# A placement table for the attention steps, half-array score and value matmuls, and reciprocals by Ln and Exp, in an attention and channel-mix kernel

## The chip, the cores and the metric

One core of one Trainium2 chip. The metric is device time in microseconds of one execution: the median of the runs shown. A profiled execution is one more run, recorded by the hardware profiler.

## What is computed

The reference, cut to what matters (B = 8, H = 8, S = 576, D = 64, 32 memory slots; channel mix 512 to 1024 to 512):

```python
a = np.exp(phi - phi.max(axis=2)); a = a / a.sum(axis=2)      # over the sequence
k_m = np.einsum('bhsm,bhsd->bhmd', a, k)
v_m = np.einsum('bhsm,bhsd->bhmd', a, v)
attn = softmax(q @ k_m.T / sqrt(64))                          # over the 32 slots
x = attn @ v_m                                                # to (B, S, 512)
xk = mu_k * x + (1 - mu_k) * x_prev                           # x_prev: one token back
xr = mu_r * x + (1 - mu_r) * x_prev
kk = np.maximum(xk @ w_k, 0)
out = sigmoid(xr @ w_r) * ((kk * kk) @ w_v)
```

## The kernel before

The eight batches go through `attention(b)`, one after the other; the 4608 tokens go through `channel_mix(c)` in nine chunks c0 to c8 of 512 tokens. Chunk c needs the tokens of batches up to c. Each chunk is 16 groups of matmuls on TensorE, one per slot: eight `key` (`pk`, L380, evicted by ScalarE's Relu L385, squared by VectorE L386), four `gate` (`pr`, L393, Tanh on ScalarE L396) and four `value` (`pv`, L404, product `o` on VectorE L407, stored by SP's queue L367). A group is four matmuls of 512 columns, or eight for `value`.

A batch's attention is a list of steps. `exp_phi` exponentiates phi (`em`). `ekv` sums em times k and v, and em times ones (`kvps`, `zps`, L193), two heads in either half of the array's columns. `norm_k` and `norm_v` divide by the sums and mask (`kbd`, `vbd`), `tr_k` and `tr_q` transpose through TensorE (`kmT`, `qT`). `scores` adds two matmuls over the full array (L252) and ScalarE exponentiates (`e`, L254). `zsum` gathers the denominators of all heads in 48 rows (`zcps`, L262), VectorE takes the reciprocal `rzf` in two bf16 parts, `spread` brings them back to 128 rows (`rbps`, L280) and multiplies (`atn`, L285). `values` gives `nops` (L294), copied by ScalarE to `x` (L296). `diff` and `mix` make `xkT` and `xrT` on VectorE (L305 to L318).

The order of work on every engine is the order in which the program issues it. The steps and the groups are interleaved by hand: the plan at the end of `attention` gives each step a slot, from batch 2 on by one plan that is stretched over 15 to 31 slots. `load_batch` puts the loads of k, q and v on POOL's queue, phi of batch 0 on SP's. The PSUM tag "at" with three buffers is shared by all attention steps; "pk" has two, "pv" three.

```python
        first = {2: 0, 3: -8}.get(b, -16)
        return [(15 - (15 - r) * (15 - first) // 31, s) for r, s in plan]
```

Of the kernel before, what the change touches and what calls it, by code (L numbers as in the profile page):

```python
# [13 lines left out]
AL = mybir.AluOpType  # L14

# [7 lines left out]
def kernel(  # L23
# [25 lines left out]
    SEG = 96  # L49
    NSEG = S // SEG  # L50
# [11 lines left out]
    identity = const.tile([128, 128], BF16, name="identity")  # L62
    make_identity(nc, identity)
# [4 lines left out]
    kmTs = [const.tile([128, 2, 2, 128], BF16, name=f"kmT{i}") for i in range(2)]  # L68
# [38 lines left out]
    for i in range(4):  # L107
        fs = slice(i * Dff // 4, (i + 1) * Dff // 4)
        nc.gpsimd.dma_start(out=wk_sb[:, :, fs], in_=wk_v[:, :, fs])
    nc.gpsimd.dma_start(out=wr_sb, in_=moe_w_r.rearrange("(do di) d2 -> di do d2", di=128))  # L110
    nc.gpsimd.dma_start(out=wv_sb, in_=moe_w_v.rearrange("(fo fi) d -> fi fo d", fi=128))
    load_batch(1)
# [8 lines left out]
    maskv = const.tile([128, 2, 2, D], BF16, name="maskv")  # L121
    nc.vector.memset(maskk, 0.0)
    nc.vector.memset(maskv, 0.0)
    for g in range(4):
        r = slice(g * M, (g + 1) * M)
        nc.vector.memset(maskk[r, g % 2, :], 1.0)
        nc.vector.memset(maskv[r, g // 2, g % 2, :], 1.0)

    NROW = H * NSEG
    selz = const.tile([128, 2 * NROW + 128], BF16, name="selz")  # L130
    nc.vector.memset(selz, 0.0)
    for g in range(4):
        nc.vector.memset(selz[g * M:(g + 1) * M, NROW + g * NSEG:NROW + g * NSEG + 1], 1.0)

    LO = 64
    KR = LO + NROW
    sel2 = const.tile([KR, NROW], BF16, name="sel2")
    nc.vector.memset(sel2, 0.0)
    nc.vector.tensor_copy(sel2[:NROW, :], identity[:NROW, :NROW])
    nc.vector.tensor_copy(sel2[LO:KR, :], identity[LO:KR, LO:KR])  # L140
    selb = const.tile([KR, 2, NSEG, 4, M], BF16, name="selb")
    for c in range(2):
        for g in range(4):
            o = c * 4 * NSEG + g * NSEG
            nc.vector.tensor_copy(
                selb[:, c, :, g, :],
                sel2[:, o:o + NSEG].unsqueeze(2).to_broadcast([KR, NSEG, M]))
    rhl2 = [const.tile([KR, SEG], BF16, name=f"rhl{i}") for i in range(2)]
    for t in rhl2:
        nc.vector.memset(t, 0.0)  # L150

    ps_mu = psum.tile([128, 2 * ND], F32, name="psmu", tag="at", bufs=3)
    nc.tensor.transpose(ps_mu, mu2, ident_f)
    mu1 = const.tile([128, 2 * ND], F32, name="mu1")
    nc.vector.tensor_scalar_add(mu1, ps_mu, -1.0)
# [3 lines left out]


    def attention(b):
        st = {}
        kv5, q5, em, kmT = kvs[b % 2], qs[b % 2], ems[b % 2], kmTs[b % 2]
# [5 lines left out]

        def ekv(parts):  # L170

            w = parts.stop - parts.start
            with_z = parts.start == 0

            def go():
                kvps = psum.tile([128, 2, w, 2 * D], F32, name="kvps", tag="at", bufs=3)
                for i in range(w):
                    st["kv"[parts.start + i]] = kvps[:, :, i, :]
                if with_z:
                    st["zps"] = psum.tile([128, 2], F32, name="zps", tag="at", bufs=3)  # L180
                for j in range(NJ):
                    for c in range(2):
                        for what in range(1 + with_z):
                            for jj in range(2):
                                pr = 2 * c + jj
                                lhsT = em[:, j].rearrange("p h m -> p (h m)")[:, pr * 64:(pr + 1) * 64]
                                if what == 0:
                                    rhs = kv5[:, parts, 2 * pr:2 * pr + 2, j, :]
                                    o = kvps[jj * 64:(jj + 1) * 64, c]
                                else:  # L190
                                    rhs = ones
                                    o = st["zps"][jj * 64:(jj + 1) * 64, c:c + 1]
                                nc.tensor.matmul(o, lhsT=lhsT, rhs=rhs, start=j == 0 and c == 0,  # L193
                                                 stop=j == NB, skip_group_check=True)
            return go

        def norm_k():
            rz = work.tile([128, 2], F32, name="rz", tag="rz")
            nc.vector.reciprocal(rz, st["zps"])
            kbd = work.tile([128, 2, 2, D], BF16, name="kbd", tag="kbd")  # L200
            for c in range(2):
                nc.vector.scalar_tensor_tensor(
                    kbd[:, c].rearrange("p h d -> p (h d)"), in0=st["k"][:, c, :],
                    scalar=rz[:, c:c + 1], in1=maskk.rearrange("p h d -> p (h d)"),
                    op0=AL.mult, op1=AL.mult)
            st["kbd"], st["rz"] = kbd, rz

        def norm_v():
            vbd = work.tile([128, 2, 2, 2 * D], BF16, name="vbd", tag="vbd")
            for c in range(2):  # L210
                nc.vector.scalar_tensor_tensor(
                    vbd[:, c], in0=st["v"][:, c].unsqueeze(1).to_broadcast([128, 2, 2 * D]),
                    scalar=st["rz"][:, c:c + 1], in1=maskv.rearrange("p j h d -> p j (h d)"),
# [7 lines left out]
        def tr_k():  # L221
# [5 lines left out]
            for c in range(2):  # L227
                for jj in range(2):
                    nc.vector.tensor_copy(kmT[:, c, jj, jj * 64:(jj + 1) * 64], ps[:, c, jj, :])  # L229
# [15 lines left out]
        def scores(c, hf):  # L245
            def go():
# [10 lines left out]
        def zsum():  # L257
            ps = psum.tile([128, SEG], F32, name="zcps", tag="at", bufs=3)
            for c in range(2):
                for sg in range(NSEG):  # L260
                    o = NROW - (c * 4 * NSEG + sg)
                    nc.tensor.matmul(ps, lhsT=selz[:, o:o + 128],  # L262
                                     rhs=st["e"][:, c, sg * SEG:(sg + 1) * SEG],
                                     start=(c == 0 and sg == 0), stop=(c == 1 and sg == NSEG - 1))
            rzf = work.tile([NROW, SEG], F32, name="rzf", tag="rzf")
            nc.vector.reciprocal(rzf, ps[:NROW, :])
            rhl = rhl2[b % 2]
            nc.vector.tensor_copy(rhl[:NROW, :], rzf)
            nc.vector.tensor_sub(rhl[LO:KR, :], rzf, rhl[:NROW, :])
            st["rhl"] = rhl  # L270

        def spread(c, hf):
            def go():
                if "at" not in st:
                    st["at"] = work.tile([128, 2, S], BF16, name="atn", tag="atn")
                ps = psum.tile([128, HALF], F32, name="rbps", tag="at", bufs=3)
                n = HALF // SEG
                for i in range(n):
                    sg = hf * n + i
                    nc.tensor.matmul(ps[:, i * SEG:(i + 1) * SEG],  # L280
                                     lhsT=selb[:, c, sg].rearrange("p g m -> p (g m)"),
                                     rhs=st["rhl"], start=(i == 0), stop=(i == n - 1),
                                     skip_group_check=True)
                sl = slice(hf * HALF, (hf + 1) * HALF)
                nc.vector.tensor_mul(st["at"][:, c, sl], st["e"][:, c, sl], ps)  # L285
            return go

        def values(pr, hf):
            def go():
                if "x" not in st:  # L290
                    st["x"] = work.tile([128, ND, S], BF16, name="x", tag="x")
                sl = slice(hf * HALF, (hf + 1) * HALF)
                ps = psum.tile([128, HALF], F32, name="nops", tag="at", bufs=3)
                nc.tensor.matmul(ps, lhsT=st["vbd"][:, pr // 2, pr % 2, :],  # L294
                                 rhs=st["at"][:, pr // 2, sl], start=True, stop=True)
                nc.scalar.copy(st["x"][:, pr, sl], ps)  # L296
# [23 lines left out]

        if b <= 1:
            at = [-1] * 5 if b == 0 else [9, 11, 12, 13, 14]
            plan = [
                (at[0] - 3, exp_phi), (at[0], ekv(slice(0, 1))), (at[0], norm_k), (at[0], tr_k),
                (at[1], tr_q(0)), (at[1], tr_q(1)), (at[1], scores(0, 0)), (at[1], scores(0, 1)),
# [93 lines left out]
    def steps_of(b):  # L421
        if b not in made:
            made[b] = attention(b)
# [41 lines left out]
```

## Time and profile before

| | |
|---|---|
| median of 3 runs | 274.89 us (274.87 to 275.49) |
| profiled execution, its own time | 274.43 us |
| its span, first to last instruction | 272.7 us |
| mean granted TensorE clock | 0.947 |
| matmuls / vector / scalar instructions | 1708 / 491 / 221 |

The span is what the profile's rows add up to; 1.7 us of the execution's own time lie outside it. Busy time counts what an engine executes, without waits; matmuls are pipelined, so the spacing of their starts tells their cost better than their durations, which include the way through the array.

### The profile page before, as it was taken

To read this page: it belongs to the slowest core of one execution; us is meant where nothing else is said; L and a number is where in the kernel's file an instruction comes from. 1 tells how busy PE (TensorE), PEld (TensorE's weight loads), DVE (VectorE), ACT (ScalarE), POOL (GpSimd) and SP (SyncE) were. 2 spreads that over 40 slices of the span, in tenths; PEclk is the share of its full clock that TensorE was granted. 3 is DMA by queue.
4 is the path that set the end of the run, shared out by engine and by line. 5 is a ranking of instruction groups with operands and counts; after the bars stand their busy time and mean duration, and the time that the engine had idled before them with its cause. 6 is when DMAs were issued, how large, how long until landed. Compare 5 with 4: busy or idle time off the path is not lost.

```text
span 272.7 us, 4541 instructions
## 1 busy us (share of the span) xinstructions
PE 227.4 (83%) x1708; PEld 117.1 (43%) x1737; DVE 169.8 (62%) x491; ACT 105.3 (39%) x221; POOL 54.4 (20%) x74
## 2 busy tenths in 40 slices
PE   0576798973999985998968897899899999999992
PEld 0442244530455442554535454545454554444441
DVE  7548743549655498545883778378829957933422
ACT  3023263130454513534525343634362472451720
POOL 8552365400262062051202400000000000000000
PEclk9996589996699998899999999999999999999998
DMA  8999999994359779739840991013001401402124
GB/s 149 187 197 217 220 223 192 244 228 74 89 67 185 176 100 188 138 35 192 150 126 2 138 237 41 0 41 105 12 2 40 114 4 38 115 9 110 38 52 102
DMA packets 49653, 31.22 MB, mean 115 GB/s; under 512 B 14824, under 2 KB 44016, under 8 KB 49632
## 3 DMA queue, kind: packets, MB, share of 16 engines
q0 software_dynamic: 42544, 20.91, 55.9%
q1 hardware_dynamic: 7088, 10.03, 13.1%
q8 instruction: 13, 0.21, 0.3%
q14 instruction: 8, 0.07, 0.1%
HBM read 38.28 MB, written 9.44 MB: 175 GB/s over the span
## 4 chain that ended last, share of the span: by engine, by line
PE 54%; DVE 23%; ACT 8%; DMA 8%; issue 5%; POOL 1%; SPq 0%; DVEq 0%; POOLq 0%
PE pk L380 17%; PE pv L404 15%; PE pr L393 8%; DMA out_dram<-o 5%; ACT x L296 4%; PE qtps L238 3%; DMA q<-in_q_dram 3%; DVE o L407 3%; DVE mu_d L317 3%; PE kvps L193 3%; PE scps L252 3%; ACT rl L385 3%; DVE sq L386 2%; DVE diff L305 2%; DVE xkT L318 2%
## 5 line engine op out<-in xcount | busy, mean ns | idle before, releaser
L380 PE MATMUL pk<-xkT,wk 128*128 128x512 bf16 x276 | 75.6, 407 | 9.8 <-DVE xkT L318 8.7
L385 ACT ACTIVATE rl<-pk 128x512 bf16<-128x512 f32 x72 | 42.5, 595 | 73.7 <-PE pk L380 69.5
L404 PE MATMUL pv<-wv,sq 128*128 128x512 bf16 x278 | 66.7, 379 | 0.5
L407 DVE SCALAR_TENSOR_TENSOR o<-th,pv 128x512 f32<-128x512 f32 x36 | 24.6, 684 | 41.1 <-PE pv L404 28.4
L380 PEld LDWEIGHTS <-wk 128*128 128x128 bf16 x288 | 27.5, 102 | 43.3 <-issue 18.5
L386 DVE TENSOR_TENSOR sq<-rl 128x512 bf16<-128x512 bf16 x72 | 29.8, 423 | 26.2 <-ACT rl L385 25.9
L404 PEld LDWEIGHTS <-sq 128*128 128x128 bf16 x288 | 27.7, 98 | 29.3 <-issue 0.2
L396 ACT ACTIVATE th<-pr 128x512 f32<-128x512 f32 x36 | 21.4, 596 | 43.9 <-PE pr L393 43.9
L393 PE MATMUL pr<-wr,xrT 128*128 128x512 bf16 x137 | 35.0, 379 | 0.8 <-issue 0.6
L296 ACT CAST x<-nops 128x288 bf16<-128x288 f32 x64 | 22.1, 407 | 14.5 <-PE nops L294 14.2
L317 DVE TENSOR_SCALAR mu_d<-diff,mu 128x576 bf16<-128x576 bf16 x64 | 22.0, 376 | 0.5
L254 ACT ACTIVATE e<-scps 128x288 bf16<-128x288 f32 x32 | 11.7, 408 | 23.6 <-PE scps L252 23.3
L393 PEld LDWEIGHTS <-xrT 128*128 128x128 bf16 x144 | 13.6, 98 | 14.9 <-issue 0.6
L238 PE MATMUL qtps<-identity,q 128*64 128x128 bf16 x320 | 15.0, 245 | 4.8 <-DVE qT L242 2.3
L252 PE MATMUL scps<-qT,kmT 128*128 128x288 bf16 x64 | 12.9, 315 | 6.4 <-DVE kmT L229 4.9
L238 PEld LDWEIGHTS <-q 128*64 128x64 bf16 x320 | 11.9, 125 | 12.4 <-issue 12.0
L242 DVE COPY qT<-qtps 128x576 bf16<-128x576 bf16 x32 | 13.3, 450 | 5.0 <-PE qtps L238 4.8
L83 POOL DMA_DIRECT2D kv<-in_k_dram x8 | 7.2, 902 | 45.0 <-PE zps L193 42.5
L294 PE MATMUL nops<-atn,vbd 128*128 128x288 bf16 x64 | 14.8, 301 | 1.5 <-ACT x L296 0.6
L193 PE MATMUL kvps<-kv,em 128*64 128x256 bf16 (+1 forms) x200 | 14.9, 272 | 1.0 <-DMA kv<-in_k_dram 0.9
L193 PEld LDWEIGHTS <-em 128*64 128x64 bf16 x360 | 12.9, 120 | 6.1 <-issue 5.5
L285 DVE TENSOR_TENSOR atn<-e,rbps 128x288 bf16<-128x288 bf16 x32 | 12.7, 447 | 1.0 <-PE rbps L280 1.0
(61 smaller groups left out, 196.3 us busy)
## 6 DMA issues: line engine op xcount, KB each, us to landing
out_dram<-o SPq DMA_DIRECT2D x40, 128.0 KB, 2.4
kv<-in_k_dram POOLq DMA_DIRECT2D x8, 512.0 KB, 7.4
q<-in_q_dram POOLq DMA_DIRECT2D x8, 512.0 KB, 9.6
kv<-in_v_dram POOLq DMA_DIRECT2D x8, 512.0 KB, 11.2
out_dram<-o SPq DMA_DIRECT2D x16, 256.0 KB, 3.0
phm<-in_phi_dram POOLq DMA_DIRECT2D x7, 512.0 KB, 10.6
wk<-in_moe_w_k_dram POOLq DMA_DIRECT2D x4, 256.0 KB, 10.8
wv<-in_moe_w_v_dram POOLq DMA_DIRECT2D x1, 1024.0 KB, 15.5
```

The costliest lines, as they stand in the source:

```text
L193: nc.tensor.matmul(o, lhsT=lhsT, rhs=rhs, start=j == 0 and c == 0, stop=j == NB, skip_group_check=True)
L238: nc.tensor.matmul(ps[i * D:(i + 1) * D, j * 128:(j + 1) * 128], lhsT=q5[:, 2 * pr + i, j, :], rhs=identity, is_transpose=True, start=True ...
L252: nc.tensor.matmul(ps, lhsT=kmT[:, c, jj, :], rhs=st["qT"][:, 2 * c + jj, sl], start=(jj == 0), stop=(jj == 1))
L296: nc.scalar.copy(st["x"][:, pr, sl], ps)
L317: nc.vector.tensor_scalar_mul(t[:, i], st["d"][:, pr + i, :], mu1[:, o:o + 1])
L380: nc.tensor.matmul(pk, lhsT=wk_sb[:, di, fi * 128:(fi + 1) * 128], rhs=xk_T[:, di, t0:t0 + CT], start=(di == 0), stop=(di == ND - 1))
L385: nc.scalar.activation(rl, pk, AF.Relu, scale=0.5 ** 0.5)
L386: nc.vector.tensor_mul(st["sq"][:, fi, :], rl, rl)
L393: nc.tensor.matmul(pr, lhsT=xr_T[:, di, t0 + ts * 128:t0 + (ts + 1) * 128], rhs=wr_sb[:, di, :], start=(di == 0), stop=(di == ND - 1))
L396: nc.scalar.activation(th, pr, AF.Tanh, scale=0.5)
L404: nc.tensor.matmul(pv, lhsT=st["sq"][:, fi, ts * 128:(ts + 1) * 128], rhs=wv_sb[:, fi, :], start=(fi == 0), stop=(fi == NF - 1))
L407: nc.vector.scalar_tensor_tensor(o, in0=st["pr"][ts], scalar=1.0, in1=pv, op0=AL.add, op1=AL.mult)
```

## The change

- Every attention step gets a slot from a table: STEADY for batches 4 to 7, FIRST for batches 0 to 3. All groups and steps are sorted by slot. The plan's stretching goes.
- `scores`: the two matmuls of a pair go to two halves of the array's columns, with 64-column weights; kmT is a tile without zeros, copied at once.
- `denom`, `recip`, `weigh`: a matmul by a block matrix of ones (`sumh`) gives each row its denominator; ScalarE takes Ln, then Exp of its negative; VectorE multiplies. `zsum` and `spread` go.
- `values`: vbd is a plain 64-column tile, and the matmuls of a pair read the two halves of the rows.
- `gate`: Exp per group, and for two groups together Ln(x + 1) and Exp of its negative, in place of Tanh; `value` multiplies by it. The factors of one half in Relu and Tanh go.
- em's sums are made in a step of their own (`esum`), with full-width weights.
- At the start: k, then q in two halves, the identity, v in two halves; w_k in two loads; one load of the table with Ln and Exp; sixteen matmuls on zeros (`keep_busy`). The last value group is computed and stored in two halves.

```diff
+STEADY = [("q0", -15), ("q3", -15), ("q2", -15), ("q1", -15), ("exp", -15), ("kv", -14), ("z", -14), ("nk",
...
+    nc.scalar.preload_act_table_set("natural_log_exp_and_others")
...
+    load_phi(0, nc.sync)
+    load_rows(kvs[0][:, 0], k[0])
+    load_rows(qs[0], q[0], 2)
+    make_identity(nc, identity)
+    load_rows(kvs[0][:, 1], v[0], 2)
...
+    def keep_busy(n):
+
+        ps = psum.tile([128, CT], F32, name="idle", tag="pk", bufs=2)
+        for _ in range(n):
+            nc.tensor.matmul(ps, lhsT=zeros[:, 0:128], rhs=zeros, start=True, stop=True,
+                             skip_group_check=True)
...
+        def esum():
+            st["zps"] = psum.tile([128, 2], F32, name="zps", tag="at", bufs=3)
+            for j in range(NJ):
+                for c in range(2):
+                    nc.tensor.matmul(st["zps"][:, c:c + 1], lhsT=heads(j, c * 128, 128), rhs=ones,
+                                     start=j == 0 and c == 0, stop=j == NB, skip_group_check=True)
...
                 for jj in range(2):
-                    nc.tensor.matmul(ps, lhsT=kmT[:, c, jj, :], rhs=st["qT"][:, 2 * c + jj, sl],
-                                     start=(jj == 0), stop=(jj == 1))
+                    nc.tensor.matmul(ps[jj * 64:(jj + 1) * 64, :], lhsT=st["kmT"][:, c, jj, :],
+                                     rhs=st["qT"][:, 2 * c + jj, sl], start=True, stop=True,
+                                     skip_group_check=True)
                 nc.scalar.activation(st["e"][:, c, sl], ps, AF.Exp, scale=scale)
...
+        def denom(c, hf):
...
+                nc.tensor.matmul(ps, lhsT=sumh.rearrange("p g m -> p (g m)"), rhs=st["e"][:, c, sl],
+                                 start=True, stop=True)
+                nc.scalar.activation(st["lz"][:, c, sl], ps, AF.Ln)
...
+        def recip(c):
+            def go():
+                nc.scalar.activation(st["lz"][:, c], st["lz"][:, c], AF.Exp, scale=-1.0)
...
+        def weigh(c):
...
+                nc.vector.tensor_mul(st["at"][:, c], st["e"][:, c], st["lz"][:, c])
...
+        def values(c, hf):
...
+                for jj in range(2):
+                    r = slice(jj * 64, (jj + 1) * 64)
+                    ps = psum.tile([128, HALF], F32, name="nops", tag="at", bufs=3)
+                    nc.tensor.matmul(ps, lhsT=st["vbd"][r, c].rearrange("p h d -> p (h d)"),
+                                     rhs=st["at"][r, c, sl], start=True, stop=True)
+                    pss.append(ps)
...
-                nc.scalar.activation(th, pr, AF.Tanh, scale=0.5)
-                st["pr"][ts] = th
+                if ts % 2 == 0:
+                    st[ts // 2] = work.tile([128, 2, Dm], F32, name="sg", tag="sg", bufs=2)
+                sg = st[ts // 2]
+                nc.scalar.activation(sg[:, ts % 2], pr, AF.Exp, scale=-1.0)
+                if ts % 2 == 1:
+                    nc.scalar.activation(sg, sg, AF.Ln, bias=1.0)
+                    nc.scalar.activation(sg, sg, AF.Exp, scale=-1.0)
...
-                nc.vector.scalar_tensor_tensor(o, in0=st["pr"][ts], scalar=1.0, in1=pv,
-                                               op0=AL.add, op1=AL.mult)
-                store(o, t0 // 128 + ts)
+                    nc.vector.tensor_mul(o[:, cols], st[ts // 2][:, ts % 2, cols], pv[:, cols])
+                    store(o, t0 // 128 + ts, cols)
```

The order of instructions is seen best at three places. First ScalarE around batch 5's scores in c3, before and in the change; th and sg are the gate, em the exponentials of phi, lz the logarithms and reciprocals:

```order
L396 ACTIVATE th<-pr 128x512 x2
L254 ACTIVATE e<-scps 128x288 x4
L385 ACTIVATE rl<-pk 128x512
L167 ACTIVATE em_81<-phm 128x8x4x32
L168 ACTIVATE em_81<-pht 64x256
L385 ACTIVATE rl<-pk 128x512 x6
```

```order
L287 ACTIVATE e<-scps 128x288
L420 ACTIVATE sg<-pr 128x512
L287 ACTIVATE e<-scps 128x288 x3
L420 ACTIVATE sg<-pr 128x512
L422 ACTIVATE sg<-sg 128x1024
L423 ACTIVATE sg<-sg 128x1024
L299 ACTIVATE lz<-zps 128x288 x2
L420 ACTIVATE sg<-pr 128x512
L304 ACTIVATE lz<-lz 128x576
L299 ACTIVATE lz<-zps 128x288
L420 ACTIVATE sg<-pr 128x512
```

The scores' Exp stood in one block behind the gates; now the gates' passes of 1024 columns and the denominators' Ln and Exp stand among them.

Second TensorE where a batch's last values meet the next batch's scores, before (gate, values, kv) and in the change (keys, values, scores, gate):

```order
L393 MATMUL pr<-wr,xrT 128x512
L294 LDWEIGHTS vbd
L294 MATMUL nops<-atn,vbd 128x288
L294 LDWEIGHTS vbd
L294 MATMUL nops<-atn,vbd 128x288
L193 LDWEIGHTS em_82
```

```order
L402 MATMUL pk<-xkT,wk 128x512
L324 LDWEIGHTS vbd
L324 MATMUL nops<-atn,vbd 128x288
L324 LDWEIGHTS vbd
L324 MATMUL nops<-atn,vbd 128x288
L284 LDWEIGHTS kmT
L284 MATMUL scps<-qT,kmT 64x288
L284 LDWEIGHTS kmT
L284 MATMUL scps<-qT,kmT 64x288
L415 LDWEIGHTS xrT
```

The listing gives the rows of the output; that nops reads 64 rows of its operands stands in the diff. The values moved from the gates to the keys of the chunk, and what follows them is a score pair in half the columns.

Third POOL's queue at the start, before and in the change:

```order
masks.py:199 AFFINE_SELECT identity<-identity 128x128
L83 DMA kv_77<-in_k_dram 128x8x256
L86 DMA kv_77<-in_k_dram 64x8x64
L83 DMA q_79<-in_q_dram 128x8x256
L86 DMA q_79<-in_q_dram 64x8x64
L83 DMA kv_77<-in_v_dram 128x8x256
```

```order
L118 DMA kv_72<-in_k_dram 128x8x256
L122 DMA kv_72<-in_k_dram 64x8x64
L118 DMA q_74<-in_q_dram 128x4x256
L122 DMA q_74<-in_q_dram 64x8x64
L118 DMA q_74<-in_q_dram 128x4x256
masks.py:197 MEMSET identity 128x128
```

The identity moved behind the loads of k and q, and q's main part is two loads of four heads.

## Rows read from the trace of the kernel before

**Rows 1.** The page, part 1: busy time, share of the span, instructions.
```profile
PE 227.4 (83%) x1708; PEld 117.1 (43%) x1737; DVE 169.8 (62%) x491; ACT 105.3 (39%) x221; POOL 54.4 (20%) x74
```

**Rows 2.** Stretches: length; busy PE, PEld, DVE, ACT, POOL; granted clock; DMA share; GB/s.
```profile
0.00:29.67 29.67, 14.77 (x146) 8.56 (x147) 19.38 (x83) 6.97 (x15) 16.45 (x26) 0.87 1.27 194
29.67:67.44 37.77, 29.55 (x219) 13.79 (x223) 20.75 (x65) 12.16 (x26) 12.64 (x16) 0.86 1.33 196
67.44:98.77 31.33, 29.65 (x275) 16.04 (x280) 19.52 (x55) 13.44 (x28) 9.56 (x13) 0.91 0.72 121
98.77:131.99 33.22, 27.43 (x211) 14.61 (x212) 22.08 (x63) 13.51 (x30) 9.39 (x12) 0.95 1.03 143
131.99:213.40 81.41, 72.12 (x595) 38.89 (x606) 58.29 (x161) 35.54 (x78) 6.30 (x8) 1.00 0.36 71
213.40:233.10 19.70, 19.34 (x111) 9.66 (x112) 14.61 (x39) 9.30 (x20) 0.00 (x0) 1.00 0.23 51
233.10:267.80 34.70, 34.54 (x158) 15.58 (x159) 14.43 (x29) 14.34 (x24) 0.00 (x0) 1.00 0.23 63
267.80:272.70 4.90, 0.00 (x0) 0.00 (x0) 0.69 (x1) 0.00 (x0) 0.00 (x0) 0.84 0.49 107
```

**Rows 3.** Timeline of TensorE in c4 and c5: start us, us, instruction, idle before.
```profile
162.46 1.03 PE L380 MATMUL pk<-xkT,wk 128*128 128x512 bf16 x4
163.42 0.75 PE L238 MATMUL qtps<-identity,q 128*64 128x128 bf16 x20
...
184.91 0.65 PE L252 MATMUL scps<-qT,kmT 128*128 128x288 bf16 x4
185.40 1.89 PE L404 MATMUL pv<-wv,sq 128*128 128x512 bf16 x7
...
188.86 0.67 PE L262 MATMUL zcps<-e,selz 128*128 128x96 bf16 x12
189.37 1.03 PE L380 MATMUL pk<-xkT,wk 128*128 128x512 bf16 x4
...
193.03 0.47 PE L238 MATMUL qtps<-identity,q 128*64 128x128 bf16 x10 [0.59 <-DVE qT L242]
```

**Rows 4.** Timeline of the first 40 us: loads, batch 0's chain, the first keys.
```profile
1.44 1.01 POOL L83 DMA_DIRECT2D kv<-in_k_dram  x1
...
9.01 0.32 PE L193 MATMUL kvps<-kv,em 128*64 128x128 bf16 x2 [0.88 <-DMA kv<-in_k_dram]
...
21.49 1.55 DVE L285 TENSOR_TENSOR atn<-e,rbps 128x288 bf16<-128x288 bf16 x4 [0.45 <-PE rbps L280]
25.27 0.58 PE L380 MATMUL pk<-xkT,wk 128*128 128x512 bf16 x1
...
29.67 0.58 PE L380 MATMUL pk<-xkT,wk 128*128 128x512 bf16 x1 [0.88 <-DVE xkT L318]
30.48 8.56 PE L380 MATMUL pk<-xkT,wk 128*128 128x512 bf16 x27 [0.22 <-issue]
...
39.85 0.88 POOL L83 DMA_DIRECT2D kv<-in_v_dram  x1 [1.53 <-DMA kv<-in_v_dram]
```

**Rows 5.** Timeline of TensorE in c4, batch 6's kv and z, then the gate.
```profile
175.07 0.30 PE L193 MATMUL kvps<-kv,em 128*64 128x256 bf16 x2
...
175.21 0.30 PE L193 MATMUL kvps<-kv,em 128*64 128x256 bf16 x2
175.32 0.20 PE L193 MATMUL zps<-ones,em 128*64 128x1 bf16 x2
175.68 0.81 PE L393 MATMUL pr<-wr,xrT 128*128 128x512 bf16 x3 [0.16 <-issue]
```

**Rows 6.** Groups of instructions, forms apart: busy us, mean ns, idle before, releaser.
```profile
L254 ACT ACTIVATE e<-scps 128x288 bf16<-128x288 f32 x32 | 11.7, 408 | 23.6 <-PE scps L252 23.3
L167 ACT ACTIVATE em<-phm 128x1024 bf16<-128x1024 f32 x8 | 8.4, 1049 | 3.2 <-DMA phm<-in_phi_dram 3.2
L167 ACT ACT_TABLE_LOAD x1 | 1.3, 1283 | 0.7 <-PEq L449 0.7
```

More of the change, by code (lines that the diff above doesn't have):

```diff
@@ L178, in go @@
                     st["kv"[parts.start + i]] = kvps[:, :, i, :]
-                if with_z:
-                    st["zps"] = psum.tile([128, 2], F32, name="zps", tag="at", bufs=3)
                 for j in range(NJ):
                     for c in range(2):
[L183 to L194, printed above, removed]
-            return go
+                        for jj in range(2):
+                            pr = 2 * c + jj
+                            nc.tensor.matmul(kvps[jj * 64:(jj + 1) * 64, c], lhsT=heads(j, pr * 64, 64),
+                                             rhs=kv5[:, parts, 2 * pr:2 * pr + 2, j, :],
+                                             start=j == 0 and c == 0, stop=j == NB,
+                                             skip_group_check=True)
+            return go
+        def esum():
[4 more added lines that the diff above has]
+                                     start=j == 0 and c == 0, stop=j == NB, skip_group_check=True)
+            st["rz"] = work.tile([128, 2], F32, name="rz", tag="rz")
+            nc.vector.reciprocal(st["rz"], st["zps"])
         def norm_k():
-            rz = work.tile([128, 2], F32, name="rz", tag="rz")
-            nc.vector.reciprocal(rz, st["zps"])
             kbd = work.tile([128, 2, 2, D], BF16, name="kbd", tag="kbd")
@@ L292, in go @@
                 sl = slice(hf * HALF, (hf + 1) * HALF)
[L293 to L296, printed above, removed]
+                pss = []
+                for jj in range(2):
+                    r = slice(jj * 64, (jj + 1) * 64)
[3 more added lines that the diff above has]
+                    pss.append(ps)
+                for jj in range(2):
+                    nc.scalar.copy(st["x"][:, 2 * c + jj, sl], pss[jj])
             return go
@@ L351, in attention @@
-        first = {2: 0, 3: -8}.get(b, -16)
-        return [(15 - (15 - r) * (15 - first) // 31, s) for r, s in plan]
-    def store(o, t):
+        two = [(0, 0), (0, 1), (1, 0), (1, 1)]
+        steps = {"exp": exp_phi, "kv": ekv(slice(0, 2)), "k": ekv(slice(0, 1)), "v": ekv(slice(1, 2)),
+                 "z": esum, "nk": norm_k, "nv": norm_v, "tk": tr_k, "load": reload, "mu": load_mu}
+        for i in range(4):
+            steps[f"q{i}"] = tr_q(i)
+            steps[f"s{i}"] = scores(*two[i])
+            steps[f"l{i}"] = denom(*two[i])
+            steps[f"d{i}"] = diff(i)
+            for w in range(2):
+                steps[f"{'kr'[w]}{i}"] = mix(w, i)
@@ new lines, in attention, with store @@
+        for i in range(2):
+            steps[f"r{i}z"] = recip(i)
+            steps[f"w{i}"] = weigh(i)
+            steps[f"d{2 * i}d"] = diff(2 * i, 2)
+            for w in range(2):
+                steps[f"{'kr'[w]}{2 * i}d"] = mix(w, 2 * i, 2)
+        steps["dd"] = diff(0, 4)
+        for i in range(4):
+            steps[f"x{i}"] = values(*two[i])
+        for i in range(1, 30):
+            steps[f"busy{i}"] = lambda i=i: keep_busy(i)
+        return steps
+    def store(o, t, cols):
@@ L371, in channel_mix @@
         t0 = c * CT
-        st = {"pr": {}}
+        st = {}
         def key(fi):
@@ L409, in go @@
-                store(o, t0 // 128 + ts)
-            return go
-        if c == 0:
-            return [key(fi) for fi in range(NF)] + [gate(t) for t in range(4)] + [
-                value(t) for t in range(4)]
-        return [key(fi) for fi in range(NF)] + [
-            gate(0), gate(1), value(0), gate(2), value(1), gate(3), value(2), value(3)]
-    made = {}
-    def steps_of(b):
-        if b not in made:
-            made[b] = attention(b)
-        return made[b]
-    for s in range(-4, 16 * NCH):
-        if s >= 0:
-            if s % 16 == 0:
-                mixing = channel_mix(s // 16)
-            mixing[s % 16]()
-        for b in range(max(0, s // 16), min(B, s // 16 + 4)):
-            for r, step in steps_of(b):
-                if r == s - 16 * (b - 1) if b > 0 else r == s:
-                    step()
+                n = 2 if c == NCH - 1 and ts == 3 else 1
@@ new lines, in value @@
+            return go
+        groups = [key(fi) for fi in range(NF)]
+        order = "g0 g1 g2 g3 v0 v1 v2 v3" if c == 0 else "g0 g1 v0 v1 g2 g3 v2 v3"
+        return groups + [(gate if o[0] == "g" else value)(int(o[1])) for o in order.split()]
+    todo = []
+    for b in range(B):
+        steps = attention(b)
+        for n, (name, pos) in enumerate(FIRST[b] if b in FIRST else STEADY):
+            todo.append((pos + 16 * (b - 1) if b > 0 else pos, b, n, steps[name]))
+    for s in range(16 * NCH):
+        if s % 16 == 0:
+            groups = channel_mix(s // 16)
+        todo.append((s, -1, 0, groups[s % 16]))
@@ L438 @@
+    for _, _, _, step in sorted(todo, key=lambda t: t[:3]):
+        step()
 _INS = ['q', 'k', 'v', 'phi', 'moe_mu_k', 'moe_mu_r', 'moe_w_k', 'moe_w_v', 'moe_w_r']
```

183 lines of the change are left out of this document (65 added, 118 removed), and 25 rows, old and new, of tables (FIRST, STEADY).

## Prediction

> **What bounds the kernel now.** I read the busy shares first: TensorE is busy 83% of the 272.7 us span, VectorE 62%, ScalarE 39% [rows 1]. A share is a mean over unlike stages, so next comes the table by stretch [rows 2]. Its cuts are the starts of the channel-mix chunks c0 to c8; c0 and c1 are cut where their last input part is ready. c7 and c8 carry no attention: 34.70 us, with TensorE busy 34.54, so a bare chunk is 17.35 us, and nine are 156. In c3 to c5 one attention batch runs beside each chunk: 81.41 us, or 27.1 each, with TensorE busy 24.0 and idle 3.1. ScalarE is busy only 11.85 per chunk there and the DMA engines 0.36. So TensorE bounds that stage, and the idle 3.1 is waits in the middle of its queue, of which the transposes waiting 0.59 us for the qT copy are one [rows 3]. In c2 the idle part is 5.8 us, in c0 8.2, ahead of c0 14.9. In c0 and c1 the granted clock averages 0.86 and 0.91: TensorE had stood idle and restarted at the lower of its two levels (1.2 of 2.4 GHz). 27 matmuls of c0 take 8.56 us where 5.8 is the full rate, which is 2.7 lost [rows 4]. Early on the loads matter too: k of batch 0 lands at 9.01, v of batch 1 at 39.85 [rows 4].
>
> The profiled execution took 274.43 us, 1.73 more than its span; the median of the runs shown is 274.89, 0.2% above. I sum against the 274.43.
>
> **TensorE's own work per batch.** Four full-width score matmuls of 288 columns take 0.49 us (184.91 to 185.40), so eight take 0.98 [rows 3]. After, each pair writes two column halves. Whether halves run side by side is seen in kvps: two matmuls of 256 columns into two halves, with two one-column ones, come every 0.14 us (175.07, 175.21) [rows 5]; 512 columns in one take 0.216 (34.70/160). So they do: four pairs cost 0.49, saved 0.49.
> Denominators: twelve zcps matmuls take 0.51 (188.86 to 189.37) [rows 3], twelve rbps at the same rate as much; four of 288 columns at 0.1225 replace both. Saved 0.53.
> Sums z: before about 0.3 (ten pairs in the 0.03 that kvps leaves); after, ten with full-width weights at the 0.042 of zcps, 0.42. Lost 0.12.
> Values: eight matmuls, 0.98. After, pairs read the two row halves. No row shows row halves: the bounds are 0.49 (side by side, as column halves) and 0.98 (one after the other). I take 0.49, since the nearest row is kvps.
> The saving is 0.49 + 0.53 - 0.12 + 0.49 = 1.4 us per batch, 11.2 in all.
>
> **Against it: changes between full and half array.** The listing has 52 before and 107 after, 6 and 13 per dense chunk; the second excerpt shows three of them in a row. The four pk matmuls from 162.46 should end their issue at 163.32; the half-width transposes start at 163.42, so one change cost 0.10 [rows 3]. The dearest such gap is the one behind z: 175.32 to 175.68, 0.36 [rows 5]. 55 more changes cost 5.5 us at 0.10; the ends are 0 and 20. I take 0.10, as the row is the plain case and 0.36 has the one-column matmuls ahead of it. The Trainium skill (TensorEngine Tiling (Array Packing), Key Properties) says that changing the tiling mode drains TensorE and gives no figure: the 0.10 agrees in kind, and by that rule the total would be no better than mine. So half of the tiling gain is paid back; the arithmetic alone nets 5.7 us, and what is left must come from waits.
>
> **ScalarE, the new cover.** 288 columns take 0.365 of busy time (11.7/32; one alone 0.408), 1024 columns 1.049 [rows 6]; between them, 576 columns are 0.65 by interpolation. Per chunk with a batch it gets four Ln of 288 (1.46), two Exp of 576 (1.30), two Ln and two Exp of 1024 (4.20); the gate's Exp takes the Tanh's place on the same shape. With 11.85 that is 18.8 us in a chunk of 23.8, and in c7 and c8 7.2 + 4.2 = 11.4 of 17.35. Nothing on the path, if Ln costs what Exp does; no row shows Ln. The bounds are the same per column and twice that, and I take the same. VectorE loses rzf, the casts and the doubled vbd, and multiplies two wide tiles in place of four PSUM ones: about 2 us less per chunk than its 19.4 (58.29/3).
>
> **The stretches.** Ahead of c0 (29.67): k is issued at about 0.75, not 1.44, as the identity moves behind the q loads (third excerpt). Sums, reciprocal, casts and spreading ahead of atn at 21.49 become one Ln and one Exp that overlap the second half's scores; q in two halves starts the transposes before it has all landed. First differences from about 19, then four diff and mix steps at 1.47 each (25.27 to 29.67 for three) [rows 4]: 25.0. The sixteen zero matmuls fill time that TensorE otherwise waits for k, and cost nothing; I count no clock gain, since the sparse stage behind them would lose it again.
> c0 (37.77): 17.35 + 2.7 clock + batch 1's 4.5 + batch 2's transposes and kv 2.9 + twelve changes 1.2 + 3 of waits, an estimate for the eight x evictions (2.8 at 0.35), which stand in one block: 31.5. Loads allow it: v of batch 2 would land near 50.6 (v of batch 1 at 39.85 plus one batch's 11 us), and is wanted near 51.
> c1 (31.33): 17.35 + batch 2's rest 1.6 + batch 3's 4.1 + fifteen changes 1.5 + 2.5 of waits (VectorE has some 23 us of work here): 27.0.
> The loads of a later batch move to just behind the transposes and kv that free their buffers. POOL's queue holds nothing but loads by then, and a batch's four land within some 11 us, well ahead of their use 24 slots on (35 us); the waits that they add delay only further loads. SP's stores keep their number but for the last, which is split.
> c2 and c3 to c5 (33.22, 81.41): 24.0 - 1.4 + seven changes 0.7 + 0.5 of waits = 23.8 each, as the table starts each batch's scores 24 slots ahead of the next chunk and puts work between each step and its reader. 23.8 and 71.4.
> c6 (19.70): only values are left, 17.35 + 0.49 + eight changes 0.8 = 18.6. c7, c8: 34.7. Tail (4.90): the last product and store are half as wide, 4.5.
> Sum: 25.0 + 31.5 + 27.0 + 23.8 + 71.4 + 18.6 + 34.7 + 4.5 = 236.5; with 1.73, **238.2 us**, 13% below 274.43. Of the 36 us, 5.7 are arithmetic and 30 are waits and cold restarts.
>
> **Rivals.**
> 1. *ScalarE becomes the bound.* It has 11.85 of old and 6.96 of new work per dense chunk and is served in order; it reaches 23.8 when the new passes cost 1.7 times my rows. For: no row shows Ln, and gate passes stand ahead of the Ln that frees a score buffer. Against: every ScalarE shape here fits one price per column. At twice the price the chunk is 25.8 and in-order waits add about 1; over c1 to c5 that is 3 x 5 = 15, less what slack takes: 250 us.
> 2. *The tiles do not give what they say*: the row halves run one after the other (8 x 0.49 = 3.9) and a change costs 0.22, the middle of its bounds (55 x 0.12 = 6.6). 238.2 + 10.5 gives 249 us. For: no row on row halves. Against: kvps.
> 3. *Slower: table reloads on ScalarE between Ln and Exp.* A load took 1.283 us [rows 6]. The new order alternates between the two 78 times, ten per dense chunk: 18.8 + 12.8 = 31.6 instead of 23.8, over six chunks +47, or 285 us. It decides from where an alternation costs 1.0 us: then ScalarE needs 29 per chunk, and the 36 us are gone. Against: the listing has a single load, at the start, as before. The Trainium skill (ScalarE: Activation LUTs, Table sets: the hidden batching unit) has exp and ln in one set, with one load; by that rule nothing is added. The trace of before has one load for Exp and Tanh, and none with Ln.
>
> **Numbers.** 0.3% is about what a measurement here can tell from no change. My forecast (TensorE bound, 230 to 245) 0.75; ScalarE bound 0.11; dear tiles 0.10; slower 0.02; nothing gained, with every removed wait replaced by another, 0.02. The low end: the waits of c0, c1 and the dense chunks vanish (3 + 2.5 + 2 = 7.5), 230.5. The high end takes in most of rivals 1 and 2: 250. Faster 0.96, same 0.01, slower 0.03.
>
> **What would show it.** Right: dense chunks of 23 to 24.5 us with TensorE idle under 1; c0's first full group at 25; score pairs starting 0.12 us apart per pair; gaps of 0.1 at array changes; Ln at Exp's duration; one table load. Wrong: ScalarE busy above 90% of a dense chunk with TensorE waiting for its evictions; value pairs 0.24 us apart; a chunk waiting for a load.

## The result and the profile after

The changed kernel takes 237.37 us (median of 4 runs, 237.32 to 238.66) where the kernel before took 274.88 beside it: a ratio of 0.8647, 95% interval 0.8611 to 0.8683. The profiled execution took 237.40 us, its span 235.6. The forecast was 238.2. Of the kernel with the new operations in the old slots, further down, two of four runs (285.75 and 286.29 us) were in a slower state with a lower granted clock and are left out.

First the busy shares of the changed kernel (the page's part 1):

```profile
PE 217.0 (92%) x1521; PEld 103.3 (44%) x1521; DVE 148.7 (63%) x381; ACT 161.7 (69%) x305; POOL 54.3 (23%) x74
```

Against [rows 1], TensorE lost 10 us of busy time but went from 83% to 92% of a shorter span: some 45 us of idle became 19. ScalarE went from 105 to 162.

Next the table by stretch, cut as in [rows 2] (c0 begins where its last input part is ready; columns: stretch, length, busy PE, PEld, DVE, ACT, POOL, granted clock, DMA share, GB/s):

```profile
0.00:24.85 24.85, 16.54 (x133) 7.33 (x134) 13.51 (x56) 9.42 (x21) 15.49 (x25) 0.83 1.24 185
24.85:56.22 31.37, 29.64 (x260) 14.69 (x259) 19.46 (x58) 19.92 (x38) 14.01 (x18) 0.92 1.46 221
56.22:83.04 26.82, 25.85 (x190) 12.17 (x188) 20.98 (x52) 21.77 (x46) 12.19 (x16) 1.00 1.47 228
83.04:106.12 23.08, 22.73 (x172) 11.08 (x171) 16.95 (x40) 17.67 (x35) 6.31 (x8) 1.00 1.21 185
106.12:176.04 69.92, 68.88 (x519) 33.76 (x517) 49.98 (x119) 55.36 (x108) 6.31 (x8) 1.00 0.40 80
176.04:194.64 18.60, 18.60 (x90) 7.86 (x88) 13.56 (x30) 14.74 (x26) 0.00 (x0) 1.00 0.25 58
194.64:229.20 34.56, 34.56 (x169) 16.37 (x167) 13.40 (x28) 22.78 (x32) 0.00 (x0) 1.00 0.21 61
229.20:235.60 6.40, 0.16 (x2) 0.00 (x0) 0.88 (x3) 0.00 (x0) 0.00 (x0) 0.93 0.34 82
```

From c3 to c5 a chunk takes 23.3 us instead of 27.1, with TensorE idle 0.35 instead of 3.1. From c1 to c8 the clock is full; before, c1 began cold. c7 and c8 are as long as before. The tail is the one stretch that grew, from 4.9 to 6.2 counted from the end of TensorE's last matmul (the last row is cut 0.16 earlier).

The first 56 us differ from one execution to the next: in a second profile of the same kernel c1 begins at 57.15 instead of 56.22. From c1's first matmul to the end both have 179.4 us, and their chunks agree to 0.01. Differences of a few tenths are therefore read from there, and not from the medians.

### The profile page after: what moved, and what is told of

Its sections match the earlier page's. It is cut to its first block, busy times and chain, and to the rows that moved or that the text cites. A ratio compares the mean times of both kernels' runs of the same rounds, so it can differ in the third digit from the quotient of the medians.

```text
span 235.6 us, 4112 instructions
## 1 busy us (share of the span) xinstructions
PE 217.0 (92%) x1521; PEld 103.3 (44%) x1521; DVE 148.7 (63%) x381; ACT 161.7 (69%) x305; POOL 54.3 (23%) x74
## 4 chain that ended last, share of the span: by engine, by line
PE 67%; DMA 15%; ACT 11%; DVE 2%; issue 2%; DVEq 0%; POOLq 0%
PE pv L434 22%; PE pk L402 21%; PE pr L415 12%; DMA q<-in_q_dram 8%; DMA wk<-in_moe_w_k_dram 4%; PE kvps L216 3%; DMA kv<-in_k_dram 3%; PE qtps L270 3%; PE nops L324 2%; ACT x L328 2%; ACT rl L406 2%; ACT lz L299 1%; ACT sg L422 1%; PE scps L284 1%; ACT sg L423 1%
## 5 line engine op out<-in xcount | busy, mean ns | idle before, releaser
L402 PE MATMUL pk<-xkT,wk 128*128 128x512 bf16 x288 | 71.0, 392 | 3.0 <-DVE xkT L350 3.0
L434 PE MATMUL pv<-wv,sq 128*128 128x512 bf16 (+1 forms) x296 | 66.3, 373 | 0.0
L407 DVE TENSOR_TENSOR sq<-rl 128x512 bf16<-128x512 bf16 x72 | 30.1, 423 | 29.2 <-ACT rl L406 29.1
L436 DVE TENSOR_TENSOR o<-sg,pv 128x512 f32<-128x512 f32 (+1 forms) x37 | 24.0, 670 | 26.8 <-ACT sg L423 24.4
L420 ACT ACTIVATE sg<-pr 128x512 f32<-128x512 f32 x36 | 21.3, 596 | 12.4 <-PE pr L415 12.4
L422 ACT ACTIVATE sg<-sg 128x1024 f32<-128x1024 f32 x18 | 19.0, 1057 | 0.6
L423 ACT ACTIVATE sg<-sg 128x1024 f32<-128x1024 f32 x18 | 19.0, 1057 | 0.6
L311 DVE TENSOR_TENSOR atn<-e,lz 128x576 bf16<-128x576 bf16 x16 | 12.0, 754 | 5.3 <-ACT lz L304 5.0
L108 POOL DMA_DIRECT2D phm<-in_phi_dram x7 | 6.4, 914 | 33.0 <-ACT em L200 28.8
L299 ACT ACTIVATE lz<-zps 128x288 f32<-128x288 f32 x32 | 12.0, 408 | 2.1 <-PE zps L297 2.0
L324 PE MATMUL nops<-atn,vbd 64*128 64x288 bf16 x64 | 11.2, 291 | 2.4 <-ACT x L328 1.4
L350 DVE TENSOR_TENSOR xkT<-x,mu_d 128x1152 bf16<-128x1152 bf16 (+1 forms) x20 | 12.8, 639 | 0.7
```

Of the source, the lines that this page charges most:

```text
L402: nc.tensor.matmul(pk, lhsT=wk_sb[:, di, fi * 128:(fi + 1) * 128], rhs=xk_T[:, di, t0:t0 + CT], start=(di == 0), stop=(di == ND - 1))
L407: nc.vector.tensor_mul(st["sq"][:, fi, :], rl, rl)
L420: nc.scalar.activation(sg[:, ts % 2], pr, AF.Exp, scale=-1.0)
L422: nc.scalar.activation(sg, sg, AF.Ln, bias=1.0)
L423: nc.scalar.activation(sg, sg, AF.Exp, scale=-1.0)
L434: nc.tensor.matmul(pv[:, cols], lhsT=st["sq"][:, fi, ts * 128:(ts + 1) * 128], rhs=wv_sb[:, fi, cols], start=(fi == 0), stop=(fi == NF - 1))
```

## Experiments

**What is worth more, the table or the operations?** Four kernels make a square. One has the changed kernel's operations in the slots of the plan before; the other has the operations before in the new table.

```diff
+    def old_slots(b):
...
-        for n, (name, pos) in enumerate(FIRST[b] if b in FIRST else STEADY):
+        for n, (name, pos) in enumerate(old_slots(b)):
```

`old_slots` returns the plan before under the new step names: scores at -3 and -2, l0 to l3 and both recips at zsum's 1, weigh at spread's 4 and 5, and so on, stretched as before.

> The changed kernel's operations in the slots of the plan before: each new step stands where the step that it replaces stood. Start-up loads and zero matmuls as in the changed kernel. My theory: the operations alone are worth about 6 us on TensorE and some 4 of the start, so 262 to 268 us, and the table the rest, 25 to 30 us. The rival, that the operations (fewer steps in each chain, fewer reciprocals) took the waits away and the table adds little: 240 to 245.

Measured: 279.48 and 280.07 us, slower than the kernel before (273.94 beside it, 271.76 to 274.59). Its waits of TensorE (who waited for whom: us in total, times, longest):

```profile
PE pk L402 <- DVE xkT L350: 10.3, 9, 2.2
PE zps L297 <- ACT lz L299: 10.1, 8, 3.7
PE scps L284 <- DVE kmT L260: 9.0, 5, 2.8
```

The first and the third are waits of the kernel before too (8.7 and 4.9 us there); the second is new. Four Ln in one slot share three "at" buffers: the fourth denominator matmul waits until ScalarE frees one, behind the gate's three passes in c1 (3.7 us) and behind phi's exponentials in a dense chunk (1.5). Both theories were too low. The operations by themselves bring nothing in the old slots, as I placed them: all four denominators stand in the one slot that `zsum` had, and no run spreads them.

The other corner (the edits of the next two experiments, before's zsum and spread, and Tanh; zsum behind the last score step, spread at weigh's slots; no zero matmuls, which the experiment on them shows to be worth nothing; em's sums, the loads at the start and the halved last value group stay as in the change):

> The counterpart of the old slots: the operations before in the new table. Scores and values over the full array, denominators by zcps, reciprocal and rbps, gate by Tanh; zsum stands behind the last score step but two slots ahead of the first product, spread with each product; no zero matmuls. My theory, that the table is worth nearly all: TensorE gets 0.53 for the denominators and 0.14 for the scores more per batch and 0.06 less for the values, so 23.9 in a dense chunk and 240 to 243 us in all. The rival, that the table needs the new operations (their chains by Ln and Exp leave VectorE free and have fewer steps): waits come back, dense chunks over 25, 250 us or more.

Measured: 249.01 us (248.79 to 249.58), ratio 0.9097 (0.9066 to 0.9127); the changed kernel took 237.66 beside it. Its c1 and a dense chunk by the same table:

```profile
59.69:91.67 31.98, 27.67 (x226) 14.94 (x229) 26.20 (x70) 14.04 (x32) 9.49 (x12) 1.00 1.22 185
...
140.37:164.45 24.08, 23.47 (x191) 12.86 (x192) 18.77 (x48) 11.87 (x26) 0.00 (x0) 1.00 0.21 45
```

The time lies between the two theories: the dense chunk is as mine had it (23.9 expected, 24.08), the total is nearly the rival's. What mine missed is the early chunks: c1 begins at 59.69, some 3 us later than in the changed kernel, and takes 5.2 us more than its 26.82, with VectorE busy 26.2 of 32. Over the whole kernel TensorE waits 4.7 us for the denominators' VectorE chain, 1.5 of it in c1:

```profile
PE rbps L344 <- DVE rhl L333: 4.7, 5, 1.4
```

The square, for c1 to c6 alone (from each kernel's first matmul of c1 to its first of c7), in us:

| | length | TensorE busy | idle |
|---|---|---|---|
| before: old operations, old slots | 170.1 | 150.3 | 19.8 |
| new operations, old slots | 176.1 | 146.7 | 29.5 |
| old operations, new table | 147.6 | 139.5 | 8.1 |
| changed: new operations, new table | 138.4 | 136.1 | 2.4 |

The table takes 22 us off these chunks with the old operations and 38 with the new ones. The new operations cost 6 in the old slots and give 9 in the table. Neither part has a worth of its own. Two limits. In the profiles of the first three rows 17 to 22 matmul records are missing, in the last none; the second profile of the changed kernel lacks 16 in these chunks and shows 3.7 us of idle, so the first three idle times are 1 to 2 us too high, while the lengths are right. And each mixed corner is one placement: a table made for the old operations, or the old slots with the denominators spread, was not run.

**Are the half-array pairs worth their changes?** One kernel puts the values back on the full array, one the scores.

```diff
...
-                    nc.tensor.matmul(ps, lhsT=st["vbd"][r, c].rearrange("p h d -> p (h d)"),
-                                     rhs=st["at"][r, c, sl], start=True, stop=True)
+                    nc.tensor.matmul(ps, lhsT=st["vbd"][:, c, jj, :],
+                                     rhs=st["at"][:, c, sl], start=True, stop=True)
```

> The changed kernel with its values over the full array again (vbd padded with zeros); nothing else differs. It has 72 changes between full and half array instead of 107. My theory: the pairs cost 8 x 0.49 = 3.9 us more and 35 changes at 0.10 fall away (3.5), so 237.8 us, within 1 us of the changed kernel. If changes cost nothing, 241.3. If a change costs 0.22, 233.6. If row halves never ran side by side, the 3.9 is not lost and it takes 233.9.

Measured: 236.95 us (236.74 to 238.05), the changed kernel 237.37 and, on another occasion, 237.66. The difference is too small for the medians, but not for the chunks: dense chunks 23.25 instead of 23.31, c6 18.25 (its row of the table follows) instead of 18.60.

```profile
175.65:193.90 18.25, 18.25 (x91) 8.59 (x89) 13.57 (x30) 14.42 (x26) 0.00 (x0) 1.00 0.25 59
```

TensorE's timeline of c6, first the changed kernel's, with the group of these matmuls (count, busy us, mean ns):

```profile
177.86 0.30 PE L324 MATMUL nops<-atn,vbd 64*128 64x288 bf16 x2
178.09 1.04 PE L402 MATMUL pk<-xkT,wk 128*128 128x512 bf16 x4
179.06 0.30 PE L324 MATMUL nops<-atn,vbd 64*128 64x288 bf16 x2
...
L324 PE MATMUL nops<-atn,vbd 64*128 64x288 bf16 x64 | 11.2, 291 | 2.4 <-ACT x L328 1.4 <-DVE vbd L243 0.6 <-DVE atn L311 0.2
```

and with full-array values:

```profile
177.38 0.41 PE L326 MATMUL nops<-atn,vbd 128*128 128x288 bf16 x2
177.62 1.03 PE L404 MATMUL pk<-xkT,wk 128*128 128x512 bf16 x4
178.49 0.41 PE L326 MATMUL nops<-atn,vbd 128*128 128x288 bf16 x2
```

The two matmuls of a half-array pair last 0.30 together, as long as one of them alone (0.29), so they start within 0.01 us of each other; the full-array pair lasts 0.41, one 0.12 behind the other. The row halves do run side by side. But around the half-array pair TensorE spends 0.23 from the pair to the next pk, 0.12 of it the pair, and another 0.11 ahead of it (178.09 + 4 x 0.216 = 178.95, pair at 179.06): 0.34 in all. Full: 0.24 and nothing ahead. Two changes at 0.10 to 0.11 cost more than the 0.12 that a pair saves. c6 pays 8 x 0.105 - 4 x 0.12 = 0.36, measured 0.35. Over c1 to c6 the full array is 0.77 us shorter.

```diff
...
-                    nc.tensor.matmul(ps[jj * 64:(jj + 1) * 64, :], lhsT=st["kmT"][:, c, jj, :],
-                                     rhs=st["qT"][:, 2 * c + jj, sl], start=True, stop=True,
-                                     skip_group_check=True)
+                    nc.tensor.matmul(ps, lhsT=st["kmT"][:, c, jj, :], rhs=st["qT"][:, 2 * c + jj, sl],
+                                     start=(jj == 0), stop=(jj == 1))
```

> The changed kernel with its scores over the full array again (kmT padded with zeros, four copies); nothing else differs. 84 changes instead of 107. My theory: 8 x 0.49 = 3.9 more, 23 changes at 0.10 less: 239.0 us. If changes cost nothing, 241.3; at 0.22 each, 236.2.

Measured: 238.09 us (237.48 to 239.74); dense chunks 23.45 instead of 23.31. The score pairs stand one and three together, so fewer changes fall on each: they gain 0.14 a batch, less than a third of their 0.49.

**The zeros at the start.**

```diff
-        for n, (name, pos) in enumerate(FIRST[b] if b in FIRST else STEADY):
+        for n, (name, pos) in enumerate([s for s in FIRST[b] if s[0] != "busy16"] if b in FIRST else STEADY):
```

> The changed kernel without the sixteen matmuls on zeros. My theory: they fill idle time and the clock gain is lost in the sparse stage behind, so 237.4 us, within 0.7. The rival, that they keep the clock up for batch 0's chain: its matmuls (some 70 pairs and 12 of 288 columns) at half the rate put 1 to 2 us on the start, 239.

Measured: 237.39 us (236.93 to 238.28): nothing, as expected.

**The tail.** In the changed kernel ScalarE's last passes and the products, in the timeline:

```profile
226.55 1.06 ACT L422 ACTIVATE sg<-sg 128x1024 f32<-128x1024 f32 x1
227.64 1.06 ACT L423 ACTIVATE sg<-sg 128x1024 f32<-128x1024 f32 x1
228.73 1.35 DVE L436 TENSOR_TENSOR o<-sg,pv 128x512 f32<-128x512 f32 x3 [3.84 <-ACT sg L423]
```

The products of values 2 and 3 all wait for the gate, although value 2 was summed by 227.45 (eight matmuls from 225.72).

```diff
-        order = "g0 g1 g2 g3 v0 v1 v2 v3" if c == 0 else "g0 g1 v0 v1 g2 g3 v2 v3"
+        order = "g0 g1 g2 g3 v0 v1 v2 v3" if c in (0, NCH - 1) else "g0 g1 v0 v1 g2 g3 v2 v3"
```

> The changed kernel with all four gates of the last chunk ahead of its values. In the changed kernel the last products wait until 228.73 us for ScalarE's Exp, Ln and Exp of the last gates, and the span ends 6.4 us after TensorE's last matmul. My theory: that chain is the new last wait of the tail; with the gates first the product of value 2 is done before the end and only half a tile stands behind the last matmul: 1.5 us less, 235.9. The rival, that the end is set by the stores on SP's queue: no change, 237.4.

Measured: 236.52 us (236.33 to 237.47), 0.9 to 1.1 below the changed kernel's two medians. Part of that is the start: from c1's first matmul to the end it is 178.8 instead of 179.4, so the edit is worth 0.6 (the tail 5.6 instead of 6.2). The products are no longer behind the gate, but the next wait is there, for the stores that free the two o buffers:

```profile
227.60 0.69 DVE L436 TENSOR_TENSOR o<-sg,pv 128x512 f32<-128x512 f32 x1 [1.31 <-DMA out_dram<-o]
229.34 0.75 DVE L436 TENSOR_TENSOR o<-sg,pv 128x256 f32<-128x256 f32 x2 [1.06 <-DMA out_dram<-o]
```

So each theory had a part: the gate was the last wait, and the stores are the one behind it. My 1.5 was too much.

**How much room has ScalarE?**

```diff
...
                     nc.scalar.activation(sg, sg, AF.Exp, scale=-1.0)
+                    for _ in range(EXTRA):
+                        nc.scalar.activation(scratch, scratch, AF.Exp, scale=-1.0)
```

> The changed kernel with two ScalarE passes over 512 columns of a scratch tile behind each pair of gates, four per chunk; their result is used nowhere. ScalarE's work per dense chunk rises from 18.5 by 2.4 to 20.9 of 23.3 us. My theory, TensorE is the bound and ScalarE has room: the dense chunks stay within 0.3 us and the whole within 2.5 (the last pass stands ahead of nothing but the tail adds nothing): 237.4 to 240. The rival, that ScalarE's order already sets the pace: the passes add their own time, 2.4 x 6 to 2.4 x 9, 252 to 259.

Measured: 242.88 us (242.25 to 243.47), over my bound by 3. Dense chunks are 23.72, 0.41 more; c1 begins 2.5 to 3.4 us later; c7 and c8, which have the passes too, are no longer than in the changed kernel. A dense chunk, and TensorE's timeline in c0, in batch 1's chain:

```profile
110.25:133.97 23.72, 22.69 (x172) 11.24 (x172) 16.09 (x39) 20.53 (x41) 6.33 (x8) 1.00 0.88 145
...
44.83 0.58 PE L300 MATMUL zps<-e,sumh 128*128 128x288 bf16 x2 [2.12 <-ACT e L290]
```

In the changed kernel the same wait is 0.28. In c0 the gates' passes stand right ahead of the scores' Exp, for which TensorE waits: there ScalarE is on the path already, whatever its share.

> The same with five passes per pair of gates, ten per chunk: 6 us more ScalarE work, 24.5 in a dense chunk of 23.3. Both theories have ScalarE as the bound now: the dense chunks at 24.5 to 26.5. It gives the price behind the point at which ScalarE takes over.

Measured: 279.28 us (one run). A dense chunk, and two waits of TensorE in it:

```profile
144.47:174.54 30.07, 25.23 (x171) 12.64 (x172) 17.22 (x40) 24.20 (x47) 0.00 (x0) 0.89 0.15 35
...
149.48 0.47 PE L273 MATMUL qtps<-identity,q 128*64 128x128 bf16 x10 [2.89 <-ACT lz L302]
151.46 1.81 PE L273 MATMUL qtps<-identity,q 128*64 128x128 bf16 x30 [1.51 <-ACT x L331]
```

ScalarE is busy 24.2 of 30.1: its work exceeds the 23.3 of a dense chunk, and yet it is idle a fifth of the time. TensorE waits for buffers that ScalarE frees behind its block of passes (the two waits above). After the first of them its granted clock falls to the lower level, 0.50 from about 150 to 157 us and 1.00 elsewhere in the chunk, which makes the mean 0.89, and ScalarE in turn waits 2.2 and 2.4 us for TensorE's keys. So 6 us of passes cost 5.5 to 6.8 in the three dense chunks, not the 1 that was missing. The passes stand in blocks of five, and no run spreads them, so how much of the price is their place and how much the limit stays open.

**The gate by Tanh again.**

```diff
...
-                nc.scalar.activation(sg[:, ts % 2], pr, AF.Exp, scale=-1.0)
-                if ts % 2 == 1:
-                    nc.scalar.activation(sg, sg, AF.Ln, bias=1.0)
-                    nc.scalar.activation(sg, sg, AF.Exp, scale=-1.0)
+                nc.scalar.activation(sg[:, ts % 2], pr, AF.Tanh, scale=0.5)
...
```

> The changed kernel with the gate by Tanh again (the factors of one half as before), everything else kept. ScalarE loses 36 passes of 1024 columns (38 us), and gets table loads where Tanh and Ln alternate: 40 in the listing instead of 1. If a load costs the 1.28 us of its row, ScalarE's dense chunk is 18.5 - 4.2 + 6.4 = 20.7, still under TensorE's 23.3, and the time stays within 237 to 243. If a switch costs 2.66, as the Trainium skill (ScalarE: Activation LUTs, What ACT_TABLE_LOAD costs) says with the drain, 27.6 in a dense chunk: 255 to 265 us.

Measured: 270.16 us (268.22 to 271.39), above both theories. The profile has 38 loads; a dense chunk (c5), and ScalarE's timeline in it:

```profile
179.41:206.86 27.45, 24.13 (x171) 11.84 (x172) 17.03 (x40) 22.14 (x39) 0.00 (x0) 0.94 0.10 38
...
198.55 1.28 ACT L299 ACT_TABLE_LOAD   x1
199.85 0.71 ACT L299 ACTIVATE lz<-zps 128x288 f32<-128x288 f32 x2
200.58 1.28 ACT L420 ACT_TABLE_LOAD   x1
202.50 0.60 ACT L420 ACTIVATE sg<-pr 128x512 f32<-128x512 f32 x1 [0.64 <-PE pr L415]
```

A switch costs 1.30 from the load's start to the next instruction (198.55 to 199.85). The Trainium skill (ScalarE: Activation LUTs, What ACT_TABLE_LOAD costs) gives 2.66 with a drain; no such drain stands in these rows, and the measurement decides. So the price was the one of my theory, and its time was wrong for another reason: I had 20.7 us of ScalarE in a dense chunk and thought it room enough; the profile has six loads there and not five, 22.14, still less than 23.3, and the chunk takes 27.45. As with the extra passes, the work in ScalarE's queue stood ahead of what TensorE waits for: its transposes wait 8.4 us in all for ScalarE's copies to `x`, against 1.4 in the changed kernel.

**Both gains together.** The changed kernel again, and with full-array values and the last gates first, on one chip:

> The changed kernel once more, beside the next two on one chip, so that differences of a few tenths can be read: 237.4 us, as before within 0.3%.

> The changed kernel with its values over the full array and with the last chunk's gates ahead of its values, the two edits that were faster alone. My theory: the array changes saved (0.06 in each dense chunk, 0.35 in c6) and the shorter tail (0.9 to 1.2) add up: 1.2 to 1.6 us below the changed kernel. If either of the two was noise of the first 56 us, 0 to 0.7 below.

Measured: 237.66 us (237.33 to 238.56; ratio 0.8684, 0.8654 to 0.8715) and 236.34 (235.56 to 237.31; ratio 0.8622, 0.8590 to 0.8654): 1.3 less, a version below both kernels, though the two intervals touch. The profiles agree: from c1's first matmul to the end 1.21 us less, 0.65 of it in c1 to c6 and 0.56 from c8 on.

## Why the prediction was right, point by point

**The bound.** TensorE, as forecast: idle 0.35 in a dense chunk, where I had allowed 0.5. For the first 56 us this is less clear: the chain of work that ended last runs there through the loads of k, w_k and q for 61% of the way in the profile shown, and through the load of q for 16% in the second one.

**The stretches.** Forecast and measured, in us: ahead of c0 25.0 and 24.85 (first differences at 19, measured 18.94); c0 31.5 and 31.37; c1 27.0 and 26.82; c2 23.8 and 23.08; c3 to c5 71.4 and 69.92; c6 18.6 and 18.60; c7 and c8 34.7 and 34.56; tail 4.5 and 6.40. The sum is right to 0.9, but terms compensate: c2 to c5 were 2.2 too long, the tail 1.9 too short. Part of the agreement at the start is luck: in the second profile the cut ahead of c0 lies at 27.00, and k was issued at 1.25, not at 0.75. In c0 and c1 TensorE idled 1.7 and 1.0 us where I had 3 and 2.5 of waits, and c1 has 19 array changes, not 15. Two slips in the working: the terms of c0 add up to 31.65, not 31.5, and the middle of 0 and 0.36 is 0.18, not the 0.22 of rival 2. Neither moves the forecast by more than 0.2.

**The tail** is the one step that failed: I took 4.5 for it because the last product and store are halved, and did not ask when the product's other operand is ready. The gate's three passes in a row replaced one Tanh, and they end at 228.70, behind TensorE's last group but one. The gates-first experiment takes 0.6 of it back; in the two kernels with one Tanh per gate (the Tanh gate, the old operations in the table) the tail is 5.2 instead of 6.2. So the passes make 1.0 of the miss of 1.7. The other 0.7 lies in the halving, which saves nothing: these two have it as well, and end no sooner behind TensorE than the kernel before with its whole last product (4.9). Why, no run shows.

**The change between full and half array** at 0.10 was well taken: 0.10 to 0.11 ahead of the value pairs, and as much behind them. TensorE's timeline of c4 shows a value pair, a change to the column halves, and the one wait that is left:

```profile
129.42 1.89 PE L402 MATMUL pk<-xkT,wk 128*128 128x512 bf16 x8
131.25 0.30 PE L324 MATMUL nops<-atn,vbd 64*128 64x288 bf16 x2
131.47 0.47 PE L270 MATMUL qtps<-identity,q 128*64 128x128 bf16 x10
132.29 1.05 PE L270 MATMUL qtps<-identity,q 128*64 128x128 bf16 x30 [0.35 <-ACT x L328]
```

The eight pk end their issue at 131.15; the pair starts at 131.25, and the transposes 0.22 later, 0.12 of it the pair. The Trainium skill (TensorEngine Tiling (Array Packing), Key Properties) says that a change of the tiling mode drains TensorE; the trace agrees in kind, with 0.10 to 0.11 us for a change. With a value pair on its own between full-array groups, two changes take back more than the halves give. My saving of 0.49 per batch is there, 6 x 0.49 = 2.9 in c1 to c6, but of the 35 changes that come with the value pairs 32 fall in these chunks, by the order of the matmuls, and take 3.4 at 0.105; the runs show 0.77 lost, 0.3 more than this count explains. For batches 0 and 1 nothing is shown, since the first 56 us move by more than the difference.

**ScalarE's prices** held. Of the changed kernel, the groups of instructions:

```profile
L422 ACT ACTIVATE sg<-sg 128x1024 f32<-128x1024 f32 x18 | 19.0, 1057 | 0.6
L299 ACT ACTIVATE lz<-zps 128x288 f32<-128x288 f32 x32 | 12.0, 408 | 2.1 <-PE zps L297 2.0
L304 ACT ACTIVATE lz<-lz 128x576 f32<-128x576 f32 x16 | 10.8, 679 | 0.3
...
L100 ACT ACT_TABLE_LOAD x1 | 1.3, 1283 | 0.7 <-PEq L470 0.7
```

Ln of 288 columns takes the 408 ns of [rows 6]'s Exp, 1024 columns 1057 against 1049, 576 columns 0.68 against 0.65. A dense chunk has 18.45 us of it, forecast 18.8. With one load, the rival of reloads fell. The rival that ScalarE becomes the bound was wrong here but nearer than I thought: 2.4 us more per chunk already cost 5.2 in all (242.88 against 237.66), half of it or more ahead of c1.

**Arithmetic and waits.** "Of the 36 us, 5.7 are arithmetic and 30 are waits" was right as a sum and wrong as a picture. The square shows the two bound up: in the old slots the new operations add 10 us of idle, in the table they remove some 4 (the missing records allowed for). What they buy in c1 can be read: with the old operations there TensorE is busy 1.8 us longer and idle 3.3 us longer, 2.1 of that waiting for VectorE's part of the denominators.

## What to carry to other kernels

Where one engine bounds a stage and still idles, count its idle time by stage before pricing any operation: here 25 of the 36 us came with the old operations kept, from where each step and load stood in the queues. Half-array matmuls paid where several stood together (the scores, 0.14 us a batch); a lone pair between full-array groups, with 0.10 to 0.11 us per change on either side, did not. When an engine's share rises from 39% to 69%, look for the places where its queue stands ahead of what the bound engine waits for, the tail among them.

## What the runs showed of the hardware that was not expected

Row halves of the array run side by side as column halves do: two matmuls of 288 columns take the 0.12 us of one. A change between the full array and a half took 0.10 to 0.11 us each way. A table switch on ScalarE cost 1.30 us from start to next start, with no further drain in the trace. And ScalarE with 1 us more work than a dense chunk has room for cost 5.5 to 6.8 us per chunk: TensorE waited behind its block of passes, restarted at the lower clock, and ScalarE then waited for TensorE.
